# A Fourier-filter and MLP kernel: two packs of the second batch's first transform stage done in the head of the kernel, from input blocks that are no longer needed

## The chip, the core and the metric

One core of one Trainium2 chip. The metric is the device time of one execution in microseconds (us). The kernel before takes 2431.64 us (median of 3 runs, 2430.45 to 2433.0).

A core has engines with a queue each, run in order: PE (TensorE, matrix products), ACT (ScalarE), DVE (VectorE), POOL (GpSimd), and SP (SyncE), which here does nothing but issue DMAs. PEld is the weight load beside PE. 16 DMA engines carry all transfers of the core.

## The reference

```python
X = np.fft.rfft(x, axis=1)                       # x: 8 batches, 3008 points, 256 channels
y = np.fft.irfft(X * (filt_r + 1j * filt_i)[None], n=3008, axis=1).reshape(24064, 256)
h = y @ w_in                                     # 256 -> 2048
P = a[0] + a[1]*h + a[2]*h**2 + a[3]*h**3
Q = 1.0 + abs(b[0])*abs(h) + abs(b[1])*h**2
out = (P / (Q + 1e-6)) @ w_out                   # 2048 -> 256
```

## The kernel before

**The transform.** 3008 = 64 x 47. Stage 1 is the 47-point DFT: the input of a batch comes as eight blocks of 512 KB, called packs here (numbers q = 0 to 7). For batches 1 to 7 a pack is `stage1_load` (one DMA), four products of 64x512 (L345), two evacuations from PSUM by ACT (L386 for batch 1) and two DMAs of 240 KB (`put_rows`, L359) into the DRAM buffer scr1. Stage 2 reads scr1, takes the 64-point DFT, the product with the filter and the inverse DFT (y and z) and writes scr2. Stage 3 (x) reads scr2 and leaves the rows xh and xl (a high and a low part) that the MLP takes.

**The MLP.** 47 tiles of 512 rows, each in 16 slices of 128 hidden channels: 752 units. A unit is six products into a PSUM bank h_u (`product_in`, L682 to L685), five ACT, four DVE and two POOL instructions that make hi_u and lo_u, and six products into the output banks (`product_out`, L760 to L763), four units later. There are six banks for h_u and for the packs, y, z and x together.

**The head.** Before the first unit, `first_batch` does batch 0 with other code: eight input blocks (512 KB each, tiles x_wi and x_wo: the first four lie in the memory of wi1, which is filled with weights later), the 47-point DFT of each (`first_dft`: 32 products, L452, and four ACT evacuations, L460, into the spectrum tiles sxh and sxl), then y and z in turn for i = 0 to 11 (L499; L521 on ACT, L522 on POOL, L525 on DVE; L582 and L584; evacuation L308). Beside this the sixteen weights, which come as 64-bit numbers, are turned into two 32-bit parts: `load` (W, one DMA of 512 KB), `bits` (B: one ACT instruction L262 and five DVE instructions L263 to L271) and `split` (T: ACT L289, POOL L290 and L291). The strings HA and HB say which of these steps, and which filter loads (F, two DMAs of 512 KB, the last one four of 256 KB) and scalar steps (S), stand behind which DFT block and behind which i. At the end of the head stand the packs 0 to 5 of batch 1 and the first two chunks of stage 3.

**What remains for the units.** Packs 6 and 7 of batch 1 are loaded at the end of the head and computed among units 3 to 5 (`conv_items`). The fifteenth and the sixteenth weight (numbers 14 and 15) are decoded by `late`, step by step: five steps of the fifteenth in unit 0, its split in unit 3, the sixteenth from unit 6 on.

**What sets the order.** The order on PE, ACT, DVE and POOL is the order of the program's calls, and that of SP too, in the head and up to unit 0. Conv steps among the units go by due times (`begin`, `due`). Every DMA, whichever engine issues it, tells of its landing on one of eight semaphores, DMAHW0 to DMAHW7, given out in turn; an issue waits until the earlier DMA on its semaphore has landed, and this wait stands in the queue of the engine that issues.

Of the kernel before, what the change touches and what calls it, by code (L numbers as in the profile page):

```python
# [32 lines left out]
LAG = 4  # L33
FIRST = 3
LOAD = dict(s=1.0, y=1.2, z=0.86, t=0.86), dict(s=1.1, y=1.1, z=.95, t=1.3)
# [12 lines left out]
HD = 14  # L48
HA = ['SWF', 'TBSWF', 'TBSWF', 'BWF', 'TBSWF', 'TB', 'W', '']
HB = ['', 'TB', '', 'TB', '', 'TBW', '', 'TB', '', 'TBW', 'W', 'TB', 'T', 'TB', 'B']  # L50
# [60 lines left out]
def conv_moe(ctx: ExitStack, tc: tile.TileContext, xp, filt, w_in, w_out, ab, mats, a1, e, sgn, outT):  # L111
# [118 lines left out]
    class Weights:  # L230
# [42 lines left out]
        def bits(self):  # L273
            k = self.i
            tags = f"a{k % RING['a']}", f"w{(k + 2) % RING['w']}", f"lo{k % RING['lo']}"
            parts = [mlp.tile([128, TT], F32, tag=x, name=f"d{x}_{k}") for x in tags]
            run(self.steps(*parts, pso.tile([128, TT], I32, tag=f"o{k % 2}", name=f"dp{k}")))

        def late(self):
            pair = conv.tile([128, 2, TT], F32, tag="raw", name=f"dt{self.i}", bufs=1)  # L280
            rf = conv.tile([128, TT], F32, tag="zw", name=f"dr{self.i}", bufs=1)
            p = conv.tile([128, 2, TT], I32, tag="oe", name=f"dp{self.i}")
            yield from self.steps(pair[:, 0], pair[:, 1], rf, p[:, 0])
            yield
            self.split()
# [41 lines left out]

    def stage1_load(b, q):

        if b == 1 and q in (0, 1, 6, 7):  # L330
            xin = ring("f2").rearrange("p (j n) -> p j n", j=2)
        else:
            xin = conv.tile([128, 2, TT], F32, tag="xin", name=f"xin{b}_{q}", bufs=XB)
        nc.sync.dma_start(xin.rearrange("p a b -> p (a b)"), xp[b, q].rearrange("p m c -> p (m c)"))
        return xin
# [19 lines left out]

    def put_rows(b, q, h, ev):

        rows = scr1[b].rearrange("(h q m) g k c -> h q (g k) m c", h=2, q=8)[h, q, :RO]
        nc.sync.dma_start(rows, ev[:RO].rearrange("p (m c) -> p m c", m=2))  # L359

# [17 lines left out]
    def first_rows(b, q, h, bank, pt, xin):  # L378

        if q in (0, 1, 6, 7):  # L380
            if h == 0:
                wide[q] = conv.tile([128, 2, TT], F32, tag="ev", name=f"s1e{b}_{q}")
            ev = wide[q][:, h]
        else:
            ev = xin[:, h]
        nc.scalar.activation(ev, pt, AF.Copy)  # L386
        banks.done(bank, 0.5)
        put_rows(b, q, h, ev)

# [400 lines left out]

    ahead, early = {}, {}

    def request(b, n):
        for q in range(len(ahead), min(n, 8)):
            ahead[q] = stage1_load(b, q)

    def conv_items(b):
        q0 = S1 if b == 1 else 0
        request(b, q0 + 2)
        for q in range(q0, 8):  # L800
            yield from stage1(b, q, ahead[q])
            request(b, q + 3)
        ahead.clear()
        for _ in range(GAP):
            yield
        run_own(None)
        yield from stage2(b)
# [29 lines left out]
    def first_batch():  # L837
# [24 lines left out]
        nc.sync.dma_start(a1_all, a1)  # L862
        for q in range(8):
            xin[q] = s.first_load(q)
            if q in (0, 2, 4, 5, 7):
                do("W")
        nc.sync.dma_start(s.mats, mats[:, 2:])
        do("FASB")
        for q in range(8):
            s.first_dft(q, xin.pop(q))  # L870
            do(HA[q])
        wi_sb.append(consts.tile([128, 2, 2, 2, TT], F32R, tag="wi1", name="wi1_sb"))
        wo_sb.append(consts.tile([128, 4, 2, TT], F32R, tag="wo1", name="wo1_sb"))
# [20 lines left out]
        for q in range(S1):  # L894
            pack = stage1(1, q, xin.pop(q))
            next(pack)
            next(pack)
            if q < 2:
                early[S1 + q] = stage1_load(1, S1 + q)
            if q == 2:  # L900
                weights[HD + 1].load()
            run(pack)
# [14 lines left out]
    def begin(b):  # L917
        return FIRST if b == 1 else end(b - 1)

# [13 lines left out]
    def pipeline(squares):  # L933
# [10 lines left out]
        for i in range(n + LAG + 2 * OG):  # L944
# [10 lines left out]
            if i == 0:  # L955
                sp.enter_context(tc.manual_schedule(engines=HEAD_SP))
                ahead.clear()
                ahead.update(dict.fromkeys(range(S1)))
                ahead.update(early)
                wlate = [weights[k].late() for k in (HD, HD + 1)]  # L960
                for _ in range(5):
                    next(wlate[0])
# [27 lines left out]
            elif i < n and not active and i >= last + PGAP:  # L990
                if gen is None and nxt < B and i >= begin(nxt):
                    gen, used = conv_items(nxt), 0
                    kind = next(gen)
                if gen and i >= due(nxt, used, kind) and all(g() for g in gate):
                    next(gen)
                    used += LOAD[nxt > 1][kind]
                    post.append("c")
# [33 lines left out]
            run_tasks(i, "end")  # L1031
            if i >= 3:
                next(wlate[i >= HP], None)
# [81 lines left out]
```

## Time and profile before

| | |
|---|---|
| median of 3 runs | 2431.64 us |
| profiled execution, its own time | 2431.18 us |
| span of its instructions | 2429.4 us |
| mean granted TensorE clock | 0.997 |
| PE busy | 2397.8 us (99%) |
| DVE, ACT, POOL busy | 2259.1 (93%), 2256.9 (93%), 1952.0 us (80%) |
| DMA | 262.56 MB, mean 108 GB/s |
| chain that ended last | PE 86%, DVE 5%, POOL 4% |

The shares of busy time are means over the whole. The head takes the first 74 us (PE's first unit begins at 74.21 us); there the engines share the time differently, and the DMA engines, idle for two thirds of the units' time, are full. So stretches of the head are read one by one. All times in rows count from the start of the span.

### The profile page before, as it was taken

The numbers are of one execution on the slowest core, as the hardware profiler recorded it, in microseconds if no ns is written. First come the engines' busy times: TensorE is split into PE (matmuls) and PEld (weight loads), VectorE is DVE, ScalarE is ACT, GpSimd is POOL, SyncE is SP. The second block draws the span as 40 slices with busy tenths as digits, with TensorE's granted clock in tenths as the row PEclk, the third lists the DMA queues.
The fourth block names the chain that finished last, engine by engine and source line by source line (L and its number), as shares of the span: only waits on it lengthen the run. The fifth ranks groups of instructions, "written<-read, shape, count | busy, mean of one in ns | idle before, by whom it ended". The sixth has DMA issues, their size and how long they took to land.

```text
span 2429.4 us, 37837 instructions
## 1 busy us (share of the span) xinstructions
PE 2397.8 (99%) x11304; PEld 1927.5 (79%) x11304; DVE 2259.1 (93%) x3553; ACT 2256.9 (93%) x4383; POOL 1952.0 (80%) x2074
## 2 busy tenths in 40 slices
PE   7999999999999999999999999999999999999998
PEld 4677778888788887888878888788877888888887
DVE  7999999999999999999999999999999999999998
ACT  6889999999999999999999999999999999999998
POOL 7788867998679986798867998589976999777776
PEclk9999999999999999999999999999999999999999
DMA  9722353322433234332343323433244320100000
GB/s 369 262 81 78 110 163 119 106 94 96 162 112 103 92 105 160 108 102 94 111 151 108 109 87 116 156 128 99 93 147 147 97 88 18 55 22 23 25 10 19
DMA packets 114359, 262.56 MB, mean 108 GB/s; under 512 B 10080, under 2 KB 38880, under 8 KB 114144
## 3 DMA queue, kind: packets, MB, share of 16 engines
q1 hardware_dynamic: 113856, 259.78, 32.4%
q8 instruction: 91, 1.49, 0.3%
q14 instruction: 124, 1.02, 0.1%
q10 hardware_dynamic: 288, 0.27, 0.0%
HBM read 159.09 MB, written 100.93 MB: 107 GB/s over the span
## 4 chain that ended last, share of the span: by engine, by line
PE 86%; DVE 5%; POOL 4%; issue 2%; DMA 1%; ACT 1%; SPq 0%; DVEq 0%; POOLq 0%; ACTq 0%
PE o L760 13%; PE o L762 12%; PE o L763 12%; PE h_u L682 12%; PE h_u L683 12%; PE h_u L685 12%; PE x L640 4%; POOL q_u L741 2%; PE s L345 2%; DVE h_u L744 1%; POOL zw L562 1%; DVE hi_u L736 1%; PE y L499 1%; DVE h_u L727 1%; PE z L578 1%
## 5 line engine op out<-in xcount | busy, mean ns | idle before, releaser
L741 POOL TENSOR_TENSOR q_u<-q_u,hi_u 128x512 f32<-128x512 f32 x752 | 974.4, 1296 | 408.2 <-DVE hi_u L736 389.0
L760 PE MATMUL o<-hi_u,wo_sb 128*128 128x512 f32 x1504 | 611.8, 407 | 0.0
L744 DVE SCALAR_TENSOR_TENSOR h_u<-h_u,words_sb,q_u 128x512 f32<-128x512 f32 x752 | 564.2, 750 | 37.1 <-POOL q_u L741 35.6
L682 PE MATMUL h_u<-xh,wi_sb 128*128 128x512 f32 x1504 | 588.5, 391 | 5.7 <-ACT s1e L386 3.9
L683 PE MATMUL h_u<-xl,wi_sb 128*128 128x512 f32 x1504 | 586.6, 390 | 0.2
L762 PE MATMUL o<-lo_u,wo_sb 128*128 128x512 f32 x1500 | 585.8, 390 | 0.8 <-DVE lo_u L750 0.8
L763 PE MATMUL o<-hi_u,wo_sb 128*128 128x512 f32 x1504 | 586.3, 390 | 0.0
L722 POOL TENSOR_SCALAR q_u<-q_u,words_sb 128x512 f32<-128x512 f32 x752 | 579.8, 771 | 6.0 <-ACT a_u L707 5.8
L736 DVE SCALAR_TENSOR_TENSOR hi_u<-h_u,words_sb,a_u 128x512 fp32r<-128x512 f32 x752 | 558.6, 743 | 26.7 <-ACT a_u L712 21.8
L727 DVE SCALAR_TENSOR_TENSOR h_u<-w_u,words_sb,h_u 128x512 f32<-128x512 f32 x752 | 560.7, 746 | 0.0
L690 ACT ACTIVATE q_u<-h_u 128x512 f32<-128x512 f32 x752 | 455.6, 606 | 103.5 <-PE h_u L685 75.5
L750 DVE TENSOR_TENSOR lo_u<-h_u,a_u 128x512 fp32r<-128x512 f32 x752 | 513.0, 682 | 0.1
L707 ACT ACTIVATE a_u<-q_u 128x512 f32<-128x512 f32 x752 | 485.0, 645 | 0.0
L712 ACT ACTIVATE a_u<-a_u 128x512 f32<-128x512 f32 x752 | 478.7, 637 | 0.0
L703 ACT ACTIVATE q_u<-q_u 128x512 f32<-128x512 f32 x752 | 478.3, 636 | 0.0
L685 PE MATMUL h_u<-xh,wi_sb 128*128 128x512 f32 x1504 | 463.8, 390 | 0.0
L697 ACT ACTIVATE w_u<-h_u 128x512 f32<-128x512 f32 x752 | 452.9, 602 | 0.5 <-POOL wi_sb L291 0.5
L760 PEld LDWEIGHTS o<-hi_u,wo_sb 128*128 128x128 f32 x1504 | 282.5, 188 | 93.2 <-issue 39.1
L682 PEld LDWEIGHTS h_u<-xh,wi_sb 128*128 128x128 f32 x1504 | 282.7, 188 | 71.8 <-DVE lo_u L750 7.2
L763 PEld LDWEIGHTS o<-hi_u,wo_sb 128*128 128x128 f32 x1504 | 282.5, 188 | 60.5
L683 PEld LDWEIGHTS h_u<-xl,wi_sb 128*128 128x128 f32 x1504 | 282.8, 188 | 60.0 <-DVE xl L654 0.8
L685 PEld LDWEIGHTS h_u<-xh,wi_sb 128*128 128x128 f32 x1504 | 282.9, 188 | 59.3
(121 smaller groups left out, 2042.4 us busy)
## 6 DMA issues: line engine op xcount, KB each, us to landing
scr<-s1e SPq DMA_DIRECT2D x96, 480.0 KB, 4.7
f_sb<-filt SPq DMA_DIRECT2D x168, 256.0 KB, 3.7
xin<-scr SPq DMA_DIRECT2D x78, 512.0 KB, 4.0
xin<-xp SPq DMA_DIRECT2D x52, 512.0 KB, 3.4
tl<-scr SPq DMA_DIRECT2D x64, 384.0 KB, 3.4
outT<-oe SPq DMA_DIRECT2D x46, 512.0 KB, 2.9
scr<-ev SPq DMA_DIRECT2D x42, 512.0 KB, 2.9
raw<-w_in SPq DMA_DIRECT2D x7, 512.0 KB, 9.9
```

Source lines behind the costliest of these rows:

```text
L682: nc.tensor.matmul(o, w_in_part(0, f, cc), xh[:, cc, ts], start=cc == 0, stop=False)
L683: nc.tensor.matmul(o, w_in_part(0, f, cc), xl[:, cc, ts], start=False, stop=False)
L685: nc.tensor.matmul(o, w_in_part(1, f, cc), xh[:, cc, ts], start=False, stop=cc == 1)
L722: nc.gpsimd.tensor_scalar(out=self.q, in0=self.q, scalar1=AIK, scalar2=SGN, op0=ALU.mult, op1=ALU.add)
L727: v.scalar_tensor_tensor(out=H, in0=w, scalar=PK, in1=H, op0=ALU.add, op1=ALU.mult)
L736: nc.vector.scalar_tensor_tensor(out=self.hi, in0=self.H, scalar=self.p0, in1=self.a, op0=ALU.add, op1=ALU.mult)
L741: nc.gpsimd.tensor_tensor(out=self.q, in0=self.q, in1=self.hi.bitcast(F32), op=ALU.mult)
L744: nc.vector.scalar_tensor_tensor(out=self.H, in0=self.H, scalar=self.p0, in1=self.q, op0=ALU.add, op1=ALU.subtract)
L750: nc.vector.tensor_tensor(out=self.lo, in0=self.H, in1=self.a, op=ALU.mult)
L760: nc.tensor.matmul(o, w_out_part(0, f, dd), self.hi, start=f == 0, stop=False)
L762: nc.tensor.matmul(o, w_out_part(0, f, dd), self.lo, start=False, stop=False)
L763: nc.tensor.matmul(o, w_out_part(1, f, dd), self.hi, start=False, stop=f == 15 and not last)
```

## The change

Packs 6 and 7 of batch 1 move into the head. Pack 6 is loaded into the block of input block 0 as soon as the DFT of that block is done, pack 7 into the block of input block 1. Their products stand behind the DFT of block 6 and of block 7, their results go back into the same memory, and the four DMAs that write them to scr1 are issued by ACT. The eighth input block and the table `mats` are loaded after block 0's DFT, the filter loads move back by one place, and one `bits` step moves from behind block 5 to behind block 7. Among the units batch 1 begins with stage 2, at unit 5 in place of 3, with the same due times for y and z. The fifteenth weight takes its scratch from a PSUM bank, and its fifth step moves from unit 0 to unit 1. `bits` takes another of the three w tiles for each weight.

```diff
--- before.py
+++ after.py
@@ -31,7 +31,7 @@
 EZ = slice(0, 3 * N2), slice(2 * N2, 6 * N2), slice(5 * N2, 8 * N2)
 DFF = 2048
 LAG = 4
-FIRST = 3
+FIRST, START = 3, 5
 LOAD = dict(s=1.0, y=1.2, z=0.86, t=0.86), dict(s=1.1, y=1.1, z=.95, t=1.3)
 REST = 3
 XF = 1
@@ -46,7 +46,7 @@
 XB, FB = 4, 3
 MINW = float(np.array(897 << 20, np.int32).view(np.float32))
 HD = 14
-HA = ['SWF', 'TBSWF', 'TBSWF', 'BWF', 'TBSWF', 'TB', 'W', '']
+HA = ['SW', 'TBSFWF', 'TBSWF', 'BWF', 'TBSWF', 'TF', '', 'BW']
 HB = ['', 'TB', '', 'TB', '', 'TBW', '', 'TB', '', 'TBW', 'W', 'TB', 'T', 'TB', 'B']
 XI = {6: (2, 3), 8: (0, 4), 9: (5,), 10: (1,)}
 RAWS = ("oe", "tl", "oe", "tl", "raw", "oe", "tl", "oe", "tl", "raw", "oe", "oe", "raw", "f1", "f2", "f1")
@@ -272,15 +272,18 @@
 
         def bits(self):
             k = self.i
-            tags = f"a{k % RING['a']}", f"w{(k + 2) % RING['w']}", f"lo{k % RING['lo']}"
+            tags = f"a{k % RING['a']}", f"w{(k + 1) % RING['w']}", f"lo{k % RING['lo']}"
             parts = [mlp.tile([128, TT], F32, tag=x, name=f"d{x}_{k}") for x in tags]
             run(self.steps(*parts, pso.tile([128, TT], I32, tag=f"o{k % 2}", name=f"dp{k}")))
 
         def late(self):
             pair = conv.tile([128, 2, TT], F32, tag="raw", name=f"dt{self.i}", bufs=1)
             rf = conv.tile([128, TT], F32, tag="zw", name=f"dr{self.i}", bufs=1)
-            p = conv.tile([128, 2, TT], I32, tag="oe", name=f"dp{self.i}")
-            yield from self.steps(pair[:, 0], pair[:, 1], rf, p[:, 0])
+            if self.i == HD:
+                p = pso.tile([128, TT], I32, tag="o0", name=f"dp{self.i}")
+            else:
+                p = conv.tile([128, 2, TT], I32, tag="oe", name=f"dp{self.i}")[:, 0]
+            yield from self.steps(pair[:, 0], pair[:, 1], rf, p)
             yield
             self.split()
 
@@ -325,9 +328,11 @@
 
 
 
-    def stage1_load(b, q):
-
-        if b == 1 and q in (0, 1, 6, 7):
+    def stage1_load(b, q, home=None):
+
+        if home is not None:
+            xin = home.rearrange("p (j n) -> p j n", j=2)
+        elif b == 1 and q in (0, 1):
             xin = ring("f2").rearrange("p (j n) -> p j n", j=2)
         else:
             xin = conv.tile([128, 2, TT], F32, tag="xin", name=f"xin{b}_{q}", bufs=XB)
@@ -353,10 +358,10 @@
             else:
                 first_rows(b, q, h, k, pt, xin)
 
-    def put_rows(b, q, h, ev):
+    def put_rows(b, q, h, ev, engine=None):
 
         rows = scr1[b].rearrange("(h q m) g k c -> h q (g k) m c", h=2, q=8)[h, q, :RO]
-        nc.sync.dma_start(rows, ev[:RO].rearrange("p (m c) -> p m c", m=2))
+        (engine or nc.sync).dma_start(rows, ev[:RO].rearrange("p (m c) -> p m c", m=2))
 
     tasks = []
     pieces, gate, stages, wide = [], [], [], {}
@@ -377,7 +382,7 @@
 
     def first_rows(b, q, h, bank, pt, xin):
 
-        if q in (0, 1, 6, 7):
+        if q in (0, 1):
             if h == 0:
                 wide[q] = conv.tile([128, 2, TT], F32, tag="ev", name=f"s1e{b}_{q}")
             ev = wide[q][:, h]
@@ -385,7 +390,7 @@
             ev = xin[:, h]
         nc.scalar.activation(ev, pt, AF.Copy)
         banks.done(bank, 0.5)
-        put_rows(b, q, h, ev)
+        put_rows(b, q, h, ev, nc.scalar if q >= S1 else None)
 
     def split_rows(b, q, h, bank, pt):
 
@@ -788,22 +793,22 @@
 
     nt = B * S // T
 
-    ahead, early = {}, {}
+    ahead = {}
 
     def request(b, n):
         for q in range(len(ahead), min(n, 8)):
             ahead[q] = stage1_load(b, q)
 
     def conv_items(b):
-        q0 = S1 if b == 1 else 0
-        request(b, q0 + 2)
-        for q in range(q0, 8):
-            yield from stage1(b, q, ahead[q])
-            request(b, q + 3)
-        ahead.clear()
-        for _ in range(GAP):
-            yield
-        run_own(None)
+        if b > 1:
+            request(b, 2)
+            for q in range(8):
+                yield from stage1(b, q, ahead[q])
+                request(b, q + 3)
+            ahead.clear()
+            for _ in range(GAP):
+                yield
+            run_own(None)
         yield from stage2(b)
 
     def run(gen):
@@ -860,15 +865,22 @@
         nc.scalar.preload_act_table(AF.Abs_reciprocal_sqrt)
         nc.scalar.dma_start(ab_sb, ab.rearrange("(o n) -> o n", o=1).broadcast_to([128, 12]))
         nc.sync.dma_start(a1_all, a1)
-        for q in range(8):
+        for q in range(7):
             xin[q] = s.first_load(q)
-            if q in (0, 2, 4, 5, 7):
+            if q in (0, 2, 4, 5, 6):
                 do("W")
-        nc.sync.dma_start(s.mats, mats[:, 2:])
-        do("FASB")
+        do("ASB")
+        packs = {}
         for q in range(8):
             s.first_dft(q, xin.pop(q))
+            if q < 2:
+                packs[q] = stage1_load(1, S1 + q, raw_x[0][:, q])
+            if q == 0:
+                xin[7] = s.first_load(7)
+                nc.sync.dma_start(s.mats, mats[:, 2:])
             do(HA[q])
+            if q > 5:
+                run(stage1(1, S1 + q - 6, packs.pop(q - 6)))
         wi_sb.append(consts.tile([128, 2, 2, 2, TT], F32R, tag="wi1", name="wi1_sb"))
         wo_sb.append(consts.tile([128, 4, 2, TT], F32R, tag="wo1", name="wo1_sb"))
         load_scales()
@@ -895,8 +907,6 @@
             pack = stage1(1, q, xin.pop(q))
             next(pack)
             next(pack)
-            if q < 2:
-                early[S1 + q] = stage1_load(1, S1 + q)
             if q == 2:
                 weights[HD + 1].load()
             run(pack)
@@ -955,10 +965,8 @@
             if i == 0:
                 sp.enter_context(tc.manual_schedule(engines=HEAD_SP))
                 ahead.clear()
-                ahead.update(dict.fromkeys(range(S1)))
-                ahead.update(early)
                 wlate = [weights[k].late() for k in (HD, HD + 1)]
-                for _ in range(5):
+                for _ in range(4):
                     next(wlate[0])
             if i == SPN:
                 sp.close()
@@ -988,8 +996,8 @@
                 post.append("x")
                 xlast = i
             elif i < n and not active and i >= last + PGAP:
-                if gen is None and nxt < B and i >= begin(nxt):
-                    gen, used = conv_items(nxt), 0
+                if gen is None and nxt < B and i >= (START if nxt == 1 else begin(nxt)):
+                    gen, used = conv_items(nxt), (8 - S1) * LOAD[0]["s"] * (nxt == 1)
                     kind = next(gen)
                 if gen and i >= due(nxt, used, kind) and all(g() for g in gate):
                     next(gen)
@@ -1029,7 +1037,7 @@
             for name, lag in ORDER[CPOS:]:
                 step(lag, name)
             run_tasks(i, "end")
-            if i >= 3:
+            if i in (1, 3) or i >= HP:
                 next(wlate[i >= HP], None)
             if stages[0].b > 1:
                 stages[0].may_split()
```

The next fences show the built programs' order, row by row; a name with a number is one buffer, and the brackets name what an instruction waits for. First ACT, at the end of the DFT blocks (s1_0_6 and s1_0_7 are the PSUM banks of input blocks 6 and 7, raw5 the sixth weight, y_0_0 the first y), before:

```order
L262 ACTIVATE da1_5_505<-raw5_209 128x512 [waits DMAHW2_49,Activation_49]
L460 ACTIVATE sxh_112<-s1_0_6_0_515 128x16x12 [waits PE_49]
L460 ACTIVATE sxl_113<-s1_0_6_0_515 128x16x12
L460 ACTIVATE sxh_112<-s1_0_6_1_534 128x16x12 [waits PE_49]
L460 ACTIVATE sxl_113<-s1_0_6_1_534 128x16x12
L460 ACTIVATE sxh_112<-s1_0_7_0_555 128x16x12 [waits PE_49]
...
L460 ACTIVATE sxl_113<-s1_0_7_1_574 128x16x12
L225 TENSOR_LOAD words_sb_91 [waits Pool_49] x4
L521 ACTIVATE y0_0_601<-y_0_0_599,mats0_111 128x256 [waits DMAHW7_49,PE_49]
```

and now (s1_1_6 and s1_1_7 are the banks of packs 6 and 7):

```order
L465 ACTIVATE sxl_113<-s1_0_6_1_526 128x16x12
L391 ACTIVATE x_wi_78<-s1_1_6_0_545 128x512 [waits DMAHW6_49,PE_49]
L364 DMA scr1_1_92<-x_wi_78 120x2x256 [waits DMAHW5_49,Activation_49]
L391 ACTIVATE x_wi_78<-s1_1_6_1_546 128x512 [waits PE_49]
L364 DMA scr1_1_92<-x_wi_78 120x2x256 [waits DMAHW6_49,Activation_49]
L465 ACTIVATE sxh_112<-s1_0_7_0_555 128x16x12 [waits PE_49]
...
L465 ACTIVATE sxl_113<-s1_0_7_1_574 128x16x12
L262 ACTIVATE da1_5_593<-raw5_206 128x512 [waits DMAHW1_49]
L391 ACTIVATE x_wi_78<-s1_1_7_0_605 128x512 [waits DMAHW2_49,PE_49]
L364 DMA scr1_1_92<-x_wi_78 120x2x256 [waits DMAHW1_49,Activation_49]
L391 ACTIVATE x_wi_78<-s1_1_7_1_606 128x512 [waits PE_49]
L364 DMA scr1_1_92<-x_wi_78 120x2x256 [waits DMAHW4_49,Activation_49]
```

Four evacuations and four DMA issues have come in; the first pair stands ahead of block 7's evacuations, the second pair ahead of the first y. Each issue waits for a DMAHW semaphore.

Second SP, the loads behind the eighth weight (raw7), before (f1 and f2 are filter tiles, f0_5 the four pieces of the last filter):

```order
L438 DMA f2_1_sb_89<-filt 128x1024 [waits DMAHW2_49]
L255 DMA raw8_393<-w_in 128x1024 [waits DMAHW3_49,DVE_49,Activation_49]
L438 DMA f1_2_sb_87<-filt 128x1024 [waits DMAHW4_49]
L438 DMA f2_2_sb_90<-filt 128x1024 [waits DMAHW5_49]
L255 DMA raw9_454<-w_in 128x1024 [waits DMAHW6_49,DVE_49,Activation_49]
L438 DMA f0_5_0_456<-filt 128x512 [waits DMAHW7_49]
L438 DMA f0_5_2_458<-filt 128x512 [waits DMAHW0_49]
```

and now:

```order
L443 DMA f1_1_sb_86<-filt 128x1024 [waits DMAHW4_49]
L443 DMA f2_1_sb_89<-filt 128x1024 [waits DMAHW5_49]
L255 DMA raw9_454<-w_in 128x1024 [waits DMAHW6_49,DVE_49,Activation_49]
L443 DMA f1_2_sb_87<-filt 128x1024 [waits DMAHW7_49]
L443 DMA f2_2_sb_90<-filt 128x1024 [waits DMAHW0_49]
L443 DMA f0_5_0_499<-filt 128x512 [waits DMAHW1_49]
...
L443 DMA f0_5_3_502<-filt 128x512 [waits DMAHW4_49]
L255 DMA raw10_603<-w_out 128x2x512 [waits DMAHW7_49,DVE_49,Activation_49]
```

The two pack loads have moved the filters back by one place: the second tile of the fourth filter (f2_1) is now the last load ahead of the tenth weight (raw9), where the second tile of the fifth (f2_2) was. The last users of DMAHW5, 6, 1 and 4 ahead of ACT's issues are f2_1, raw9, f0_5_0 and f0_5_3.

Third PE, from unit 3 to the first output product, before:

```order
L685 MATMUL h_u3_1056<-xh_874,wi0_sb_76 128x512 x2
L345 MATMUL s1_1_6_0_1063<-f2_0_sb_88,a1_sb_83 64x512 [waits DMAHW4_49,PE_49]
...
L345 MATMUL s1_1_6_1_1064<-f2_0_sb_88,a1_sb_83 64x512 [waits PE_49]
...
L682 MATMUL h_u4_1093<-xh_874,wi0_sb_76 128x512 [waits Activation_49]
L683 MATMUL h_u4_1093<-xl_875,wi0_sb_76 128x512
...
L685 MATMUL h_u4_1093<-xh_874,wi0_sb_76 128x512 x2
L345 MATMUL s1_1_7_0_1100<-f2_1_sb_89,a1_sb_83 64x512 [waits DMAHW7_49,Activation_49]
...
L345 MATMUL s1_1_7_1_1101<-f2_1_sb_89,a1_sb_83 64x512 [waits DVE_49]
...
L760 MATMUL o0_0_1106<-hi_u0_1043,wo0_sb_77 128x512
```

and now:

```order
L690 MATMUL h_u3_1076<-xh_896,wi0_sb_76 128x512 x2
L687 MATMUL h_u4_1102<-xh_896,wi0_sb_76 128x512 [waits PE_49]
L688 MATMUL h_u4_1102<-xl_897,wi0_sb_76 128x512
L687 MATMUL h_u4_1102<-xh_896,wi0_sb_76 128x512
L688 MATMUL h_u4_1102<-xl_897,wi0_sb_76 128x512
L690 MATMUL h_u4_1102<-xh_896,wi0_sb_76 128x512 x2
L765 MATMUL o0_0_1109<-hi_u0_1063,wo0_sb_77 128x512 [waits DVE_49]
...
L687 MATMUL h_u5_1133<-xh_896,wi0_sb_76 128x512 [waits PE_49]
```

The packs have gone from between the units, and unit 4 no longer waits for an ACT evacuation; the first output product stands right behind it.

## Rows read from the trace of the kernel before

**Rows 1.** Busy us (count): PE, PEld, DVE, ACT, POOL; then PEclk, DMA, GB/s.
```profile
30.00:35.00 5.00, 4.61 (x7) 2.02 (x8) 1.73 (x5) 2.41 (x8) 2.46 (x2) 0.66 1.04 415
...
45.00:50.00 5.00, 4.64 (x12) 2.04 (x12) 4.76 (x10) 3.09 (x7) 4.92 (x5) 1.00 1.03 380
...
85.00:90.00 5.00, 4.48 (x17) 2.55 (x17) 3.83 (x6) 4.54 (x9) 3.83 (x4) 0.66 1.07 310
...
100.00:2420.00 2320.00, 2313.17 (x10545) 1873.68 (x10544) 2173.78 (x3407) 2180.33 (x4225) 1878.76 (x1986) 1.00 0.30 98
```

**Rows 2.** Timeline of ACT, 27 to 68 us: start, duration, what [idle before, releaser].
```profile
27.24 0.66 ACT L262 ACTIVATE da<-raw 128x512 f32<-128x512 f32 x1 [1.73 <-DMA raw<-w_in]
...
29.14 0.55 ACT L460 ACTIVATE sxh<-s 128x192 f32<-128x192 f32 x1
...
66.14 2.05 ACT L386 ACTIVATE s1e<-s 128x512 f32<-128x512 f32 x4
```

**Rows 3.** Timeline of SP's issues, 0 to 14 us.
```profile
1.20 0.42 SPq L443 DMA_DIRECT2D x_wi<-xp  x1
...
6.03 0.33 SPq L443 DMA_DIRECT2D x_wo<-xp  x1
```

**Rows 4.** DMA issues at 1.20, 30.90, 32.23, 33.41 us: size, us to landing.
```profile
x_wi<-xp SPq DMA_DIRECT2D x1, 512.0 KB, 4.8
...
f_sb<-filt SPq DMA_DIRECT2D x1, 512.0 KB, 10.0
...
raw<-w_in SPq DMA_DIRECT2D x1, 512.0 KB, 9.9
...
f<-filt SPq DMA_DIRECT2D x1, 256.0 KB, 9.4
```

**Rows 5.** Timeline of SP's issues, 26 to 40 us.
```profile
28.45 0.33 SPq L255 DMA_DIRECT2D raw<-w_in  x1
29.63 1.60 SPq L438 DMA_DIRECT2D f_sb<-filt  x2
32.23 0.33 SPq L255 DMA_DIRECT2D raw<-w_in  x1
33.41 4.11 SPq L438 DMA_DIRECT2D f<-filt  x4
```

**Rows 6.** ACT's queue instructions of L225 and L784: ns min/median/max, first and last start.
```profile
L225 ACTq TENSOR_LOAD <-words_sb x4: 275/280/473, 29.5 to 30.7; - x4
...
L784 ACTq DMA_DIRECT2D outT<-oe x1: 358/358/358, 2423.9 to 2423.9; - x1
```

**Rows 7.** Timeline, the first y and the last y products on POOL.
```profile
32.46 0.84 ACT L521 ACTIVATE y<-y,mats 128x256 f32<-128x256 f32 x2 [1.78 <-PE y L499]
...
33.38 1.27 POOL L522 TENSOR_TENSOR f<-f,y 128x512 f32<-128x512 f32 x1 [2.18 <-ACT y L521]
...
59.09 2.51 POOL L522 TENSOR_TENSOR f<-f,y 128x512 f32<-128x512 f32 x2
```

**Rows 8.** Timeline, units 0 to 5.
```profile
75.83 1.31 DVE L263 TENSOR_SCALAR dp<-f_sb 128x512 int32<-128x512 int32 x1 [0.28 <-DMA scr<-xin]
...
78.32 0.60 ACT L697 ACTIVATE w_u<-h_u 128x512 f32<-128x512 f32 x1 [0.46 <-POOL wi_sb L291]
...
81.12 0.74 DVE L727 SCALAR_TENSOR_TENSOR h_u<-w_u,words_sb,h_u 128x512 f32<-128x512 f32 x1
...
82.32 0.65 ACT L712 ACTIVATE a_u<-a_u 128x512 f32<-128x512 f32 x1
...
85.52 0.79 PE L682 MATMUL h_u<-xh,wi_sb 128*128 128x512 f32 x1 [3.87 <-ACT s1e L386]
...
89.43 0.50 PE L760 MATMUL o<-hi_u,wo_sb 128*128 128x512 f32 x1
```

**Rows 9.** DVE groups by form, 74 to 112 us, then 6 to 72 us: busy us, mean ns.
```profile
L269 DVE TENSOR_SCALAR dp<-dt 128x512 int32<-128x512 int32 x2 | 1.1, 536 | 0.0
...
L269 DVE TENSOR_SCALAR dp<-dw 128x512 int32<-128x512 int32 x14 | 9.7, 695 | 0.5
```

## The prediction

> **What bounds the kernel now.** I read the windows first, to see which engine is full in which stretch. From 100 us on PE is: 2313.17 of 2320 us [rows 1]. There the end moves by what PE is given or spared, and by when it gets going. In the head it is otherwise. From 30 to 65 us the row of 45 to 50 us is typical: POOL 4.92 and DVE 4.76 of 5, and the DMA engines full [rows 1]. Next I read the timelines of the head's ends: when the first y product leaves (ACT's L521 at 32.46 us), when the first unit stalls (PE idle 3.87 us until 85.52) and when the first output product starts (89.43 us) [rows 7, 8]. After that PE hardly stops. So the sum has two terms: how much later the y stage begins, and how much sooner after it the first output product comes. Last I read SP's issues and landings, since the change puts DMAs into ACT's queue.
>
> **SP's waits, which ACT now has as well.** The sixth input block is issued at 6.03 us; the first, on the same semaphore eight issues before, was issued at 1.20 and took 4.8 us, so it landed at 6.0 [rows 3, 4]. From then on eight transfers are on their way at any time, a load takes 10 us from issue to landing and the issues come 1.26 us apart: three steps from 28.45 to 32.23 us [rows 4, 5]. An ACT instruction that waits holds all behind it: for the sixth weight ACT stood 1.73 us until 27.24, with evacuations ready behind it [rows 2].
>
> **First term: the four scr1 writes on ACT.** The first one, of pack 6, waits for DMAHW5, whose earlier user is f2_1, the second tile of the fourth filter. When does that land? Up to f2_1 the new SP order has 27 loads of 512 KB: eight input blocks, two packs, nine weights, eight filter tiles. Up to f2_2 the old one has 27 too: eight, nine and ten. The DMA engines are full all the way, so f2_1 takes f2_2's place: issued 30.90 us (the second of the pair that begins at 29.63), landing after 10.0 us, at 40.9 [rows 4, 5]. The tenth weight follows in both, 32.23 and 9.9, at 42.2 [rows 4, 5]. ACT has the first write in its queue at about 26 us, behind the evacuations of block 6, and stands there for some 15 us.
>
> From there, step by step. Issue 0.36 us (the only DMA issue late on ACT, L784), at 41.3 [rows 6]; second evacuation of pack 6, 0.51 us (four in 2.05), at 41.8 [rows 2]; second write, when the tenth weight lands at 42.2, done 42.5. Block 7's four evacuations took from 29.14 to 30.68, 0.55 us for the first row and the rest at the same step, so 44.1 [rows 2]; L262 of the sixth weight and the first evacuation of pack 7: 45.1. Its write waits for f0_5_0, the first quarter of the last filter. In the old order that comes right behind the tenth weight (33.41 plus 9.4, 42.8) [rows 4, 5]; in the new one the two tiles of the fifth filter stand between, 2.5 us: 45.3. The two writes of pack 6 share the engines with it: 480 KB at 1.26 us per 512 KB, 1.2 us. So it lands between 45.3 and 46.5. The last wait is for f0_5_3, three quarters of 256 KB later (1.9 us) and beside one more write (0.6 us): 47.2 to 49.0. I take 48.4, nearer to the upper end because full engines must carry the added bytes. The issue (0.36) and the four register loads of L225 (29.5 to 30.7 plus 0.28, 1.5 us) follow [rows 6]: the first L521 starts at 50.3 us, against 32.46. That is 17.8 later; with the ends of the landing 16.5 to 18.4.
>
> Two sentences on the notes. The Trainium skill, page "DMA: Bandwidth & Descriptors", section "Anatomy of one DMA", says that DMA engines do not wait on semaphores and that any wait happens on the issuing sequencer before dispatch; the trace agrees for SP (6.03 us beside 6.0), and no row shows it for ACT. By that rule the sum is the one here; if the wait lay with the transfer, it would be the first rival's.
>
> **Does the y stage give any of it back?** POOL carries the stage from its first product, 33.38 us, to the last, 59.09 plus 2.51, 61.6 [rows 7]. In those 28.2 us it is free for 0.4, between the first two y, where it waited for ACT; now PE has four y products ready when ACT comes free, and this 0.4 goes. PE's low clock in 30 to 35 us (0.66 in the mean) [rows 1] falls into ACT's wait as well. Nothing else gets shorter: the y and z products, the weight steps and POOL's order in the stage are the same, and the loads come earlier than needed. What follows up to the first unit (the packs 0 to 5, the first x chunks) is paced by ACT and by events. So the first unit starts 17.4 us later (16.1 to 18.0). The eight products of each pack cost nothing in the head: PE waits for ACT there.
>
> **Second term: the first units.** By the old clock. Unit 0's DVE instruction L727 started at 81.12 us, behind five steps of the fifteenth weight that began at 75.83 [rows 8]. Now four steps stand ahead of it, with the scratch in PSUM, as for the earlier weights, where such a step takes 0.70 us (L269 there) [rows 9]: 75.83 plus 2.9 is 78.7. Its operand is there: ACT's L697 lost 0.46 us to POOL at 78.32 [rows 8], the w tile's last user, and the new tags free that tile two weights earlier. The fifth step and unit 0's L736 end at 80.8. Unit 1's L736 then waits for ACT's L712, 82.32 plus 0.65, less 0.46: 82.5 [rows 8]. Four DVE steps of 0.68 to 0.75 later, at 85.2, unit 0's lo_u is ready. PE has nothing left between unit 4 and the first output product, which starts at 85.2 in place of 89.43: 4.2 us sooner. In this are the two packs' products, two PE waits and four ACT evacuations. Against it stands the clock. PE stood still for 3.87 us and the granted clock fell, 0.66 in the mean from 85 to 90 us [rows 1, 8]; half of unit 4 and a pack ran slowly. PE now stands 3.3 us; if it runs at half clock after that for as long, it loses 1.6 us on products that bind. So 2.6 to 4.2; I take 3.2, since it is not certain that the shorter stop brings the low clock.
>
> The Trainium skill, page "VectorE: DVE Perf Modes", section "Why PSUM operands drop a tier", speaks against the PSUM scratch: fp32 there runs at the plain rate. The trace agrees for L269, 536 ns with the late scratch in SBUF and 695 in PSUM [rows 9], so one step loses 0.16 to 0.26 us; the first step took 1.31 us in SBUF [rows 8], so the five together still gain.
>
> The start of batch 1's second stage at unit 5 in place of 3, and the changed filter tiles, cost nothing I can find: y and z keep their due times, and the filters' loads come with a DMA load that is 2 MB lighter. Bound 0.5 us either way.
>
> **Sum.** 17.4 - 3.2 is 14.2 us. On the profiled execution's 2431.18 us, which stands 0.5 us below the median of the runs, that gives 2445.4 us. With the bounds of the terms, 11.4 (16.1 - 4.2 - 0.5) to 15.9 (18.0 - 2.6 + 0.5): 2442.6 to 2447.1.
>
> **Rivals.**
> 1. *The writes do not hold ACT* (not slower). Then ACT pays four issues and four evacuations, 1.4 and 2.0 us, and no longer stands 1.73 us for the sixth weight ahead of block 6 [rows 2, 6]: the y stage begins about 2 us later, and 3.2 come back: 2430. It decides wherever the issue leaves ACT before 30 us. For it: no row shows ACT waiting for a landing before it issues. Against it: the wait stands in ACT's row as in SP's, and SP is seen to wait. 7%.
> 2. *The y stage is paced by transfers*, which then have a lead of 8 us or more: DMA is full through 45 to 50 us [rows 1]. If 5 to 8 us came back, 2438 to 2440. Against it: POOL has no more than 0.4 us free. 9%.
> 3. *The landings slip further*: ACT's writes have short rows (1 KB) and could delay the last filter's quarters by more than their bytes, and the eleventh weight waits for ACT too. 3 to 6 us more: 2449 to 2451. 12%.
> 4. *The change does not do what it says*, the packs staying among the units: the order shows them gone. Below 1%.
>
> **Chances.** My forecast has 72%. Half of 3 and most of 2 go into the range: 2438.5 to 2450.0. About 0.2% (4.9 us) is what a measurement of this kernel can tell from no change. Faster than that only if 1 holds with more than its sum: 4%; within it, the rest of 1 and an extreme of 2: 7%; slower: 89%.
>
> **What would show it.** ACT idle for about 15 us from 26 to 41 us, released by a filter's landing, then shorter waits up to about 48 us; the first L521 near 50 us; POOL's y stage again 28 us long; the first unit near 91.6 us (74.21 in the timeline before plus 17.4) and the first output product about 11 us later. Wrong if ACT runs through block 7's evacuations by 32 us, if the y stage takes less than 25 us, or if the first output product comes 15 us after the first unit as before.

## The result and the profile after

The changed kernel takes 2447.79 us (median of 6 runs, 2445.26 to 2451.24), the kernel before 2432.24 in the same comparison: ratio 1.0068, 95% interval 1.0057 to 1.0078. That is 15.6 us slower. The profiled execution was the slowest of the six, 2451.24 us (span 2449.3); a second profile of the same kernel, called *again* below, has a span of 2446.3 and stands nearer to the median.

First the windows of the kernel after, from the profiled execution (columns as in [rows 1]).

```profile
30.00:35.00 5.00, 4.15 (x72) 3.21 (x72) 0.00 (x0) 0.58 (x1) 2.04 (x2) 0.74 1.03 412
35.00:40.00 5.00, 0.00 (x0) 0.00 (x0) 0.00 (x0) 0.00 (x0) 0.00 (x0) 0.60 1.03 420
...
55.00:60.00 5.00, 5.00 (x7) 1.90 (x7) 4.78 (x9) 3.39 (x8) 4.92 (x5) 0.51 0.00 0
...
85.00:90.00 5.00, 2.95 (x20) 0.89 (x16) 4.60 (x8) 2.19 (x5) 3.27 (x3) 0.72 0.56 208
90.00:95.00 5.00, 5.00 (x32) 1.53 (x24) 1.05 (x2) 3.34 (x8) 0.00 (x0) 0.60 0.76 223
...
100.00:2440.00 2340.00, 2328.40 (x10614) 1884.93 (x10614) 2192.03 (x3434) 2201.72 (x4264) 1895.93 (x2001) 1.00 0.31 99
```

From 35 to 40 us no compute engine does anything, while the DMA engines are full; from 55 to 60 us it is the reverse, and no byte moves. The loads that were spread over the y stage before now wait for it on SP. What stopped the engines stands in ACT's timeline:

```profile
41.12 0.58 ACTq L364 DMA_DIRECT2D scr<-x_wi  x1
41.74 0.60 ACT L391 ACTIVATE x_wi<-s 128x512 f32<-128x512 f32 x1 [11.16 <-DMA f_sb<-filt]
42.37 0.33 ACTq L364 DMA_DIRECT2D scr<-x_wi  x1
...
45.78 0.32 ACTq L364 DMA_DIRECT2D scr<-x_wi  x1
...
48.82 0.32 ACTq L364 DMA_DIRECT2D scr<-x_wi  x1
...
51.84 1.57 ACT L526 ACTIVATE y<-y,mats 128x256 f32<-128x256 f32 x4 [5.09 <-DMA sgn_sb<-sgn]
```

The four writes leave at 41.12, 42.37, 45.78 and 48.82 us, the first behind a filter's landing. The first y comes 19.4 us later than before (32.46, [rows 7]). The releaser named at 51.84 is none: ACT's queue was busy with the four register loads, longer than before ([rows 6]):

```profile
L225 ACTq TENSOR_LOAD <-words_sb x4: 281/422/867, 49.2 to 51.4; - x4
```

PE, from the packs to unit 1 (to be held against [rows 8]):

```profile
87.53 1.99 PE L350 MATMUL s<-f_sb,a_sb 48*64 48x512 f32 x8 [2.05 <-ACT s1e L391]
89.27 5.98 PE L350 MATMUL s<-xin,a_sb 48*64 48x512 f32 x32
...
98.42 0.51 PE L687 MATMUL h_u<-xh,wi_sb 128*128 128x512 f32 x1
...
106.08 0.39 PE L765 MATMUL o<-hi_u,wo_sb 128*128 128x512 f32 x1
...
109.36 0.50 PE L767 MATMUL o<-lo_u,wo_sb 128*128 128x512 f32 x1 [2.90 <-DVE lo_u L755]
...
116.77 0.50 PE L767 MATMUL o<-lo_u,wo_sb 128*128 128x512 f32 x1 [1.67 <-DVE lo_u L755]
```

PE stops ahead of pack 1 (the row at 87.53) and then computes the packs at half clock (the granted clock is 0.50 from 88 to 94 us); the first unit is 24.2 us late. The first output product comes 7.7 us after the first unit, against 15.2 before, but PE stops right behind it. From the first unit to unit 12's hi_u on DVE it is 45.73 us before and 44.17 now: of those 7.5 us only 1.6 are kept. The two hi_u, before and after:

```profile
119.94 0.73 DVE L736 SCALAR_TENSOR_TENSOR hi_u<-h_u,words_sb,a_u 128x512 fp32r<-128x512 f32 x1
```

```profile
142.59 0.73 DVE L741 SCALAR_TENSOR_TENSOR hi_u<-h_u,words_sb,a_u 128x512 fp32r<-128x512 f32 x1
```

### The profile page after: what moved, and what is told of

Same layout as the page of the kernel before. It is cut to its first block, busy times and chain, and to the rows that moved or that the text cites. A ratio compares the mean times of both kernels' runs of the same rounds, so it can differ in the third digit from the quotient of the medians.

```text
span 2449.3 us, 37832 instructions
## 1 busy us (share of the span) xinstructions
PE 2408.0 (98%) x11304; PEld 1932.1 (79%) x11304; DVE 2256.5 (92%) x3553; ACT 2258.2 (92%) x4383; POOL 1951.6 (80%) x2074
## 4 chain that ended last, share of the span: by engine, by line
PE 86%; DVE 4%; POOL 4%; DMA 3%; ACT 2%; issue 2%; ACTq 0%; SPq 0%; POOLq 0%; DVEq 0%
PE o L765 13%; PE o L767 12%; PE o L768 12%; PE h_u L687 12%; PE h_u L688 12%; PE h_u L690 12%; PE x L645 4%; PE s L350 2%; POOL q_u L746 2%; DVE h_u L749 1%; DVE hi_u L741 1%; PE z L587 1%; DMA f<-filt 1%; POOL zw L567 1%; DVE h_u L732 1%
## 5 line engine op out<-in xcount | busy, mean ns | idle before, releaser
L687 PEld LDWEIGHTS h_u<-xh,wi_sb 128*128 128x128 f32 x1504 | 282.3, 188 | 66.8 <-DVE lo_u L755 7.0
L767 PEld LDWEIGHTS o<-lo_u,wo_sb 128*128 128x128 f32 x1500 | 281.7, 188 | 65.7 <-DVE lo_u L755 8.5
```

The lines of the kernel that those rows point to most:

```text
L687: nc.tensor.matmul(o, w_in_part(0, f, cc), xh[:, cc, ts], start=cc == 0, stop=False)
L767: nc.tensor.matmul(o, w_out_part(0, f, dd), self.lo, start=False, stop=False)
```

## The experiments

Times of before are medians in the same comparison: 2431.0 us beside again, sp_puts, pool_puts and late_only; 2430.03 beside puts_later, sp_last, sp_order and packs_only; 2430.7 beside act7 and act6. Each ratio is to the kernel before.

**again.** No edit.

> The changed kernel once more, unaltered, for a second profile. Its profiled execution was the slowest of six (2451.24 us, median 2447.79). In that one the first y (L526) came at 51.84 us and the first unit at 98.42, 24.2 us later than before, of which 19.4 are ACT's wait and some 4.8 came after it: ACT waited 1.18 us for a weight's landing at 86.2, PE stood 2.05 us, and the packs then ran at half clock (1.05 us for a product of 512 columns in place of 0.59). Theory A: ACT's wait is the fixed part (first y again at 51.5 to 52.2) and the slow packs belong to that one execution; then the first unit comes at 94 to 96 and the time is 2446 to 2448. Rival: the slow packs are in every execution; the first unit is again at 98 and the time at the middle of the runs as well.

Measured: 2447.71 us (ratio 1.0065, 1.0052 to 1.0078).

```profile
51.45 1.57 ACT L526 ACTIVATE y<-y,mats 128x256 f32<-128x256 f32 x4 [4.87 <-DMA sgn_sb<-sgn]
```

```profile
86.79 1.09 PE L350 MATMUL s<-f_sb,a_sb 48*64 48x512 f32 x8 [2.06 <-ACT s1e L391]
87.67 3.64 PE L350 MATMUL s<-xin,a_sb 48*64 48x512 f32 x32
...
94.86 0.47 PE L687 MATMUL h_u<-xh,wi_sb 128*128 128x512 f32 x1
```

ACT's wait is the same within 0.4 us (first row), and so is PE's stop of 2.06 us, but the packs run at full clock: 3.64 in place of 5.98 us for the 32 products. The slow packs belong to the one execution, as theory A said. The first unit is 20.65 us late: 19.0 at the first y and 1.65 behind it. PE's stop ends with a landing: pack 1's load, issued at 77.59 us, took 9.1 and landed at 86.7.

```profile
f_sb<-xp SPq DMA_DIRECT2D x1, 512.0 KB, 9.1
```

**sp_puts and pool_puts.** The four writes go to another queue:

```diff
-        put_rows(b, q, h, ev, nc.scalar if q >= S1 else None)
+        put_rows(b, q, h, ev)                                    # sp_puts
+        put_rows(b, q, h, ev, nc.gpsimd if q >= S1 else None)    # pool_puts
```

> The four scr1 writes of packs 6 and 7 are issued from SP's queue, the rest as in the changed kernel. Theory A (ACT standing behind the landing of loads is what costs): ACT issues nothing and waits only for PE; by the changed kernel's trace its evacuations of pack 6, block 7 and pack 7 are done by about 35.4 us, the first y comes at 36.5 to 38 us in place of 51.84 (before: 32.46), and the time falls to 2433 to 2437. Rival B (the packs' work and bytes in the head cost as such, or the y stage waits for the later filters): the first y or the stage behind it stays late, 2443 us or more.

> The four scr1 writes are issued from POOL's queue, where they take semaphores of their own and wait for ACT's evacuation alone. Theory A: as with SP, first y at 36.5 to 38 us, 2433 to 2437 us; POOL is idle there, so up to 4 us of issuing cost nothing. Against the run with SP it tells whether the writes, held on SP until a landing, delay the loads behind them: if so this one is 1 to 2 us faster. Rival B: 2443 us or more in both.

Measured: 2433.65 us on SP (ratio 1.0007, 0.9998 to 1.0016), 2434.15 on POOL (1.0011, 1.0003 to 1.0020). Some 14 of the 16.7 us that again is slower are gone with the queue, with the same products, evacuations and bytes. ACT and then PE with the writes on SP:

```profile
30.70 1.08 ACT L391 ACTIVATE x_wi<-s 128x512 f32<-128x512 f32 x2
32.26 1.57 ACT L526 ACTIVATE y<-y,mats 128x256 f32<-128x256 f32 x4 [0.48 <-issue]
...
67.33 0.67 ACT L262 ACTIVATE da<-f_sb 128x512 f32<-128x512 f32 x1 [2.65 <-DMA f_sb<-w_in]
67.90 1.06 ACT L391 ACTIVATE s1e<-s 128x512 f32<-128x512 f32 x2
```

```profile
68.59 1.63 PE L350 MATMUL s<-f_sb,a_sb 48*64 48x512 f32 x8 [3.88 <-ACT s1e L391]
69.92 4.89 PE L350 MATMUL s<-xin,a_sb 48*64 48x512 f32 x32
...
77.98 0.50 PE L687 MATMUL h_u<-xh,wi_sb 128*128 128x512 f32 x1
```

The first y is not late at all, 0.2 us sooner than before; my 36.5 to 38 took over the half-clock DFT of the profiled execution. But the first unit is 3.8 us late. ACT's evacuation of pack 0 is named as the releaser of PE at 68.59; it stood behind L262, which waited for the fourteenth weight's landing until 67.33. Pack 1's own load, on SP and in the list of issues, landed no sooner:

```profile
60.26 0.38 SPq L339 DMA_DIRECT2D f_sb<-xp  x1
```

```profile
f_sb<-xp SPq DMA_DIRECT2D x1, 512.0 KB, 8.2
```

It landed at 68.46 (60.26 plus 8.2). So both of PE's conditions came with a landing, within 0.1 us of each other. The packs then ran at a lower clock (4.89 us in place of 3.64); that cost the first unit 0.3 us at most, for the second load of tl, which stage 3 needs, landed only at 76.23.

With POOL as the issuer the writes leave from 31.62 us on and wait for none of SP's landings: POOL's DMAs don't take the eight semaphores, which the section on the order gives to every engine. But the issuing was not free: it took until 34.8, and POOL's first y product starts only then (with SP at 33.17).

```profile
31.62 3.20 POOL L364 DMA_DIRECT2D scr<-x_wi  x4
```

The run was not 1 to 2 us faster than with SP, and pack 1's load landed at 69.7 although the writes hold no place in SP's queue. That speaks against the writes' standing on SP as the cause of the late loads, but does not rule it out, since the y stage began 1.7 us later here.

**act7 and act6.** One pack's writes stay on ACT, the other's go to SP:

```diff
+        put_rows(b, q, h, ev, nc.scalar if b == 1 and q == 7 else None)    # act7; act6: q == 6
```

> Pack 6's two writes are issued from SP, pack 7's two stay on ACT. Theory A (ACT stands until the landing of the earlier DMA on each semaphore, so the last landing sets the end, not the number of writes): ACT runs through pack 6 and block 7, then stands at pack 7's writes until the last filter's first and fourth quarter have landed, 45.1 to 45.5 and 47.1 to 48.7 us; first y at 49.5 to 51.5 us, close to the changed kernel's 51.45; 2446 to 2448 us. Rival B (each write on ACT costs a time of its own): half of the 19 us, first y near 42 us, about 2440.

> Pack 6's two writes stay on ACT, pack 7's two are issued from SP. Theory A: ACT stands at pack 6's writes until f2_1 and the tenth weight have landed (40.8 and 42.1 us), then does block 7, the weight and pack 7 in 3.6 us without a wait; with the four register loads the first y comes at 47 to 48 us, 3.5 to 4.5 sooner than in the changed kernel; 2443 to 2445 us. Rival B: as with pack 7 alone, first y near 42 us, about 2440.

Measured: act7 2448.11 us, act6 2444.40. ACT in act7, then in act6:

```profile
45.23 0.59 ACTq L364 DMA_DIRECT2D scr<-x_wi  x1
45.86 0.60 ACT L391 ACTIVATE x_wi<-s 128x512 f32<-128x512 f32 x1 [14.70 <-DMA f<-filt]
47.17 0.33 ACTq L364 DMA_DIRECT2D scr<-x_wi  x1
50.18 1.57 ACT L526 ACTIVATE y<-y,mats 128x256 f32<-128x256 f32 x4 [3.72 <-DMA sgn_sb<-sgn]
```

```profile
40.95 0.59 ACTq L364 DMA_DIRECT2D scr<-x_wi  x1
41.59 0.60 ACT L391 ACTIVATE x_wi<-s 128x512 f32<-128x512 f32 x1 [13.52 <-DMA f_sb<-filt]
42.21 0.33 ACTq L364 DMA_DIRECT2D scr<-x_wi  x1
...
45.89 0.84 ACT L526 ACTIVATE y<-y,mats 128x256 f32<-128x256 f32 x2 [0.42 <-PE y L504]
```

Two writes on ACT cost as much as four when they are the last two. A price per write is out; the landing that the last one waits for sets the end. In act6 the first y comes 1 us sooner than expected, since the register loads there (42.8 to 44.4 us) ran beside the evacuations.

**puts_later, sp_last, sp_order.** Where do sp_puts' 3.8 us come from? In puts_later pack 6's and 7's rows are written later (and hold other data: the kernel leaves out their own), in sp_last pack 1 is computed last, and in sp_order the fourteenth weight's bits step stands behind pack 3 as well:

```diff
-        put_rows(b, q, h, ev, nc.scalar if q >= S1 else None)    # in all three
+        if q < S1:                               # puts_later
+            put_rows(b, q, h, ev)
+        if q in (4, 5):
+            put_rows(b, q + 2, h, ev)
+        put_rows(b, q, h, ev)                    # sp_last and sp_order: the writes on SP
-        for q in range(S1):                      # sp_last and sp_order
+        for q in (0, 2, 3, 4, 5, 1):
-HB = ['', 'TB', '', 'TB', '', 'TBW', '', 'TB', '', 'TBW', 'W', 'TB', 'T', 'TB', 'B']   # sp_order
+HB = ['', 'TB', '', 'TB', '', 'TBW', '', 'TB', '', 'TBW', 'W', 'TB', 'T', 'TB', '']
+            if q == 3:
+                do("B")
```

> As the kernel with the writes on SP, but pack 6's and 7's rows of scr1 are written at the end of the head, behind those of packs 4 and 5 and from their results (so these rows hold other data): the 1 MB of the four writes leaves the full stretch of the DMA engines, the loads of the two packs stay in it. Theory A (bytes ahead of the late loads make them late): the fourteenth weight and pack 1's load land 0.96 MB at 0.41 MB/us, 2.3 us, sooner, at 65 and 66.1 us; first unit at 75.5 to 76, 2431 to 2432. Rival B (the late loads are held by something else than bytes, such as the store ahead of them on SP): landings as with the writes on SP, 68.4 us for pack 1, 2433.6.

> As the kernel with the writes on SP, and pack 1 is computed behind pack 5 in place of behind pack 0. In the run with the writes on SP the first y came at 32.26 us, no later than before, yet the first unit 3.8 us later (77.98): PE stood 3.88 us ahead of pack 1 at 68.59, though ACT's pack 0 evacuation, named as releaser, stood behind L262, which waited for the fourteenth weight's landing (67.25); pack 1's own load landed at 68.45. Theory A (the 2 MB of pack loads and writes moved into the full DMA engines make pack 1's load late): with other packs in between, whose loads landed by 64.7, PE goes on and the stop shrinks to what ACT's wait until 67.3 leaves, 1 to 2 us; first unit at 75.5 to 76.5, 2431 to 2432. Rival B (ACT's wait for the weight alone holds PE): the stop stays, 2433.6.

> As the kernel with pack 1 last, and the fourteenth weight's bits step (L262 on ACT, five DVE steps) stands behind pack 3 in place of ahead of pack 0, so that ACT evacuates packs 0, 2 and 3 before it waits for that weight's landing (67.25 us). Theory A: no stop of PE among the packs over 0.7 us; first unit at 74.0 to 75.0, then the ramp's 1.6 us: 2429.5 to 2431, as the kernel before or up to 1.5 us faster. Rival B (DVE's steps, now later, hold the split of the fourteenth weight and the first units): the first unit early, but units 0 to 4 give it back, 2432 to 2434.

Measured: puts_later 2429.42 us (ratio 0.9994, 0.9985 to 1.0003), sp_last 2433.37 (1.0014), sp_order 2433.69 (1.0010). PE in each of the three:

```profile
66.66 1.09 PE L350 MATMUL s<-f_sb,a_sb 48*64 48x512 f32 x8 [2.16 <-DMA f_sb<-xp]
...
75.09 0.47 PE L690 MATMUL h_u<-xh,wi_sb 128*128 128x512 f32 x1
```

```profile
74.75 3.55 PE L645 MATMUL x<-e_sb,tl 128*128 128x141 f32 x24 [2.20 <-DMA tl<-scr]
78.07 0.50 PE L687 MATMUL h_u<-xh,wi_sb 128*128 128x512 f32 x1
```

```profile
70.21 1.09 PE L350 MATMUL s<-f_sb,a_sb 48*64 48x512 f32 x8 [2.12 <-ACT xin L391]
75.00 5.26 PE L645 MATMUL x<-e_sb,tl 128*128 128x141 f32 x24 [3.71 <-DMA tl<-scr]
80.03 0.50 PE L687 MATMUL h_u<-xh,wi_sb 128*128 128x512 f32 x1
```

With 1 MB fewer ahead of them the loads of the fourteenth weight and of pack 1 land 2 us sooner (65.2 and 66.5), the first unit comes 2.9 us sooner than with sp_puts (77.98), and the time falls by 3.2 us against sp_puts by the ratios and by 4 against sp_last and sp_order, which were compared at the same time. So the writes ahead of the loads are the cost, as theory A said. It takes four issues out of SP's queue there together with their bytes; that the bytes count and not the issues rests on the full DMA engines (408 to 419 GB/s in sp_puts from 60 to 70 us) and on pool_puts. The time came out 1.6 us below what was expected.

The second half of theory A failed: with other packs put ahead, PE waits for tl, which comes behind the same queue. In sp_last the first y was 3 us late (35.29), behind a clock of 0.50 from 25 to 30 us, and the first unit was where it is in sp_puts. In sp_order it came 2 us later still: after the stop of 3.71 us the granted clock was 0.63 in the mean (75 to 80 us), and the 24 products took 5.26 us in place of 3.55. The transfers set the head's end; changing which work waits for them did not bring it forward.

**late_only and packs_only.** The second half of the change alone, and the change without it:

```diff
# late_only: these lines as the change has them; packs_only: all of them undone
-            tags = f"a{k % RING['a']}", f"w{(k + 2) % RING['w']}", f"lo{k % RING['lo']}"
+            tags = f"a{k % RING['a']}", f"w{(k + 1) % RING['w']}", f"lo{k % RING['lo']}"
...
+                p = pso.tile([128, TT], I32, tag="o0", name=f"dp{self.i}")
...
-                for _ in range(5):
+                for _ in range(4):
-            if i >= 3:
+            if i in (1, 3) or i >= HP:
```

> The kernel before with only the second half of the change: the fifteenth weight's scratch in PSUM, its fifth step in unit 1, and the other w tiles; packs 6 and 7 stay among the units and no DMA is moved. Theory A (the rearranged steps alone give what the ramp gained, 24.21 us late at the first unit and 22.65 from the eighth on): 1 to 2 us faster than before, about 2430.6. Rival: with the packs among the units PE waits for ACT's evacuation of pack 6 all the same (3.87 us idle until 85.52), and nothing changes, 2432.2.

> The changed kernel without its second half: the fifteenth weight's steps, scratch and the w tiles as before, packs 6 and 7 in the head with their writes on ACT. From unit 0's first product to the thirteenth unit's L736 it took 45.73 us before, 44.15 in the changed kernel, 45.21 with the second half alone. Theory A (the two halves add): 44.6 to 44.7 here, first y at 51.5 to 51.9, 2448.2 us. Rival B (the second half does all when the packs are gone): 45.7, 2449.3. Rival C (the packs' absence does all of the 1.6): 44.15, 2447.7.

Measured: late_only 2430.54 us (ratio 0.9997, 0.9989 to 1.0006), packs_only 2448.36. Unit 0's first product to unit 12's hi_u: 45.2 us with late_only (75.10 to 120.30), 44.7 with packs_only (95.20 to 139.94). Read so, of the 1.6 us the rearranged steps give 0.5 and the absent packs 1.0, and they add. But these are single profiles, and the same stretch took 43.8 us (puts_later) to 44.7 (pool_puts) in kernels that have both halves, so the split is not firm. The 1 to 2 us that late_only was to gain are not shown: its time can't be told from that of the kernel before, its first unit came 0.9 us later, and PE's stop is not gone ([rows 8] had 3.87):

```profile
85.83 0.54 PE L685 MATMUL h_u<-xh,wi_sb 128*128 128x512 f32 x1 [3.26 <-ACT s1e L389]
```

None of these kernels is measurably faster than the one before; the intervals of pool_puts, sp_last (1.0005 to 1.0023) and sp_order (1.0001 to 1.0019) lie just above 1.

## Why the prediction came out right, and where its steps did not

The forecast was 2445.4 us, within 2438.5 to 2450.0; 2447.8 was measured. The main mechanism, ACT standing behind landings, was right. But 2447.8 lies above the bounds of the sum itself (2442.6 to 2447.1) and only inside the range that the rivals had widened.

*ACT behind the landings: right.* The writes were forecast at 40.9, 42.2, 45.3 to 46.5 and 47.2 to 49.0 us plus the time to see each; they left at 41.12, 42.37, 45.78 and 48.82. sp_puts, act6 and act7 show that this wait, and not the packs' work, makes some 14 us. Rival 1 is out.

*The register loads: too small.* "The four register loads of L225 (... 1.5 us)" took 2.6 (2.3 in again), and the last write left at the upper end: the first y came at 51.84 (51.45 in again), not 50.3. That is 19.0 to 19.4 us late, above my 18.4.

*The y stage: right.* POOL's stage took 27.8 us (52.75 to 80.52, its first to its last y product), 0.4 less than before, as forecast. PE's low clock did not pass within ACT's wait, though: the clock was 0.51 still from 55 to 60 us. POOL covered it.

*"What follows up to the first unit ... is paced by ACT and by events": wrong.* It is paced by transfers, and lost 1.65 us (again) or 4.8 (the profiled execution, 3.2 of it by the clock). "The loads come earlier than needed" did not hold: ACT stood 1.18 us for the fourteenth weight and PE until pack 1's load had landed. I had the mechanism only as rival 2 and only as a gain. In sp_puts, where ACT does not wait, the first unit is 3.8 us late by it. Its size is not firm: from the first y to the first unit act7 took 0.5 us more than the kernel before and packs_only 2.0, and late_only, where no transfer was moved, 0.8.

*The ramp (the first units): the term was 3.2 us and measured 1.6.* Unit 0's lo_u was forecast 11.0 us after the first unit and came at 10.9 (the stop that ends at 109.36). But the first output product takes hi_u, not lo_u: it left at 7.7, and PE stopped for lo_u right behind it. The step that failed is the count itself: I took the first output product as the end of the ramp, as if nothing behind it would wait. PE's stop of 3.87 us turned into one of 2.9 and more. In the stretch up to unit 12 DVE and ACT are both busy for over nine tenths of the time; the columns are those of [rows 1], before and after:

```profile
74.21:119.94 45.73, 41.22 (x182) 31.09 (x182) 42.35 (x64) 42.15 (x81) 33.52 (x33) 0.96 0.81 261
```

```profile
98.42:142.59 44.17, 38.57 (x166) 29.62 (x166) 40.28 (x65) 40.14 (x77) 33.38 (x33) 1.00 0.70 201
```

In the profiled execution PE had 2.65 us less to do, and the stretch got 1.6 us shorter, no more than DVE's and ACT's work did (2.1 and 2.0). That DVE and ACT set its length is read from these rows; no run tests it by itself. The clock's 1.6 us, which the forecast held against the gain, did not count either: in again the clock fell behind this stop (0.66 from 105 to 110 us), in the profiled execution it did not, and both took 44.1 to 44.2 us.

The sum, for again: 20.65 at the first unit, less 1.6 in the ramp, 19.05 at unit 12, where 14.2 was forecast. All three errors (1.2 at the first y, some 2 from there to the first unit, with the 0.4 of the y stage in it, and 1.6 in the ramp) make the kernel slower than forecast; they add up to 4.85 us, and none makes good for another. That the total came so near is in part luck: behind unit 12, where the forecast has no term, 2.1 us came off. A fall of the clock in the one profile of the kernel before, told in the last section, is 1.6 of it, and smaller differences are 0.5; 16.9 is the difference of the spans, and 15.6 and 16.7 us are those of the medians in the two comparisons.

## What to carry to other kernels

A DMA issued from ACT, as from SP, brings along the wait for its semaphore's earlier transfer; here, with full DMA engines, ACT stood 11.2 to 14.8 us for one issue, and all work queued on ACT stood behind it. That is longer than the 10 us of a load: in again ACT was ready at 26.7 us, and SP issued the earlier transfer only at 30.8. Before DMAs are moved to another queue, look up what each waits for and when that lands; and when a wait has been taken away, ask which transfers were late behind it. A gain read at one instruction counts only if what comes next does not wait for an engine that is busy all the time.

## What was not expected of the hardware

*The same stop of PE, with and without a fall of the clock.* After a stop of 2.05 us the packs ran at half clock in the profiled execution, and after one of 2.06 at full clock in again, which is the same kernel. Something like it stands late in the program, between different kernels: at the corresponding place PE had stopped 1.50 us before and 1.37 in again; the windows behind it, before and then again:

```profile
1815.00:1820.00 5.00, 4.68 (x14) 3.69 (x15) 4.13 (x7) 5.00 (x11) 2.62 (x3) 0.66 0.94 312
```

```profile
1835.00:1840.00 5.00, 5.00 (x23) 4.12 (x23) 4.85 (x8) 5.00 (x11) 2.26 (x4) 1.00 0.97 316
```

One granted 0.66 in the mean and lost 1.6 us against the other. None of the other eleven profiles has a fall there, but their stops are all shorter (1.12 to 1.39 us), so in this case it may be the stop's length and not chance. The first pair shows that a single profile can hold a fall that another of the same kernel does not: two profiles of one kernel are needed before a difference of 2 to 4 us is put down to the change. What decides it, these runs do not show.

*Writes from ACT and POOL overtake loads from SP.* In the changed kernel ACT's first write of 240 KB, issued at 41.12 us, landed after 5.8 us, at 46.9; SP's 256 KB of 39.81 took 8.9, to 48.7. In pool_puts the four writes, issued from 31.62 us, landed in 7.3 us in the median; SP's load of 30.91 us took longer than the 10.0 of [rows 4]. With the writes on SP (sp_puts) they landed in the order of issue. POOL's writes and SP's load:

```profile
scr<-x_wi POOLq DMA_DIRECT2D x4, 240.0 KB, 7.3
...
f_sb<-filt SPq DMA_DIRECT2D x1, 512.0 KB, 12.6
```
